# A plan that counts TensorE's instructions, and whole tiles stored at the end

## The chip, the cores and the metric

The kernel runs on one core of a Trainium2 chip. The metric is the device time of one execution in microseconds, the median over runs; lower is better. Before the change the median of three runs is 1213.6 us (1208.06, 1213.6, 1229.15).

## What is computed

A recurrent attention over 4 batches x 8 heads x 768 steps with a 40x40 state, then two feed-forward layers over the 3072 rows of 320 numbers:

```python
def _attn_ref(r, k, v, w, a, b):
    ...
    for t in range(S):
        y[:, :, t] = np.einsum('bhd,bhde->bhe', rt, state)
        Sa = np.einsum('bhde,bhe->bhd', state, at)
        state_decay = state * wt[:, :, None, :] - np.einsum('bhd,bhe->bhde', Sa, bt)
        state = state_decay + np.einsum('bhd,bhe->bhde', vt, kt)

x = attention as (B * S, H * D)                  # 3072 x 320
h = np.maximum(x @ w_in, 0.0); x = h * h @ w_out  # d_ff 2048
g = x @ w_gate; out = (g * sigmoid(g)) * (x @ w_val) @ w_out2   # d_ff 1536
```

## The kernel before

The recurrence is worked in chunks of 32 steps, so that almost everything is a product on TensorE: small float32 products of 16 to 64 columns on parts of the array (lines 802 to 1072, the stages x, v, p, u, s, t, z, c, y, S, k of the code). The profile shows a float32 product as two matmuls, each with a weight load. The two layers are split into high and low parts in the faster float32r format: the input products of the first layer (L460, 256 columns), its output products (L465, 320 columns), the same for the second layer (L460 with 512 columns, L1472).

All of this is put in order by a planner, `Plan`, when the program is built. Each step is an `op` with a cost for each engine that may take it, the keys it reads and writes, and a due time. `step` takes the engine that is free first, `choose` picks among the steps that are ready there, by due time, with rules that keep TensorE's clock up and avoid changes of the array's shape; `pe_time` gives a TensorE step its time. The result is one fixed order for each engine, in which the steps' functions emit their instructions. The first layer's products stand between the small products of the attention from about 185 us on; what is left of them when the attention is done covers the time in which the second layer's weights are loaded.

The second layer runs in six blocks of 512 rows (`pair2`): for each of 12 slices of 128 hidden columns, a gate product and a value product (`f_in`, eight matmuls each), the gate function on ACT and DVE (L1461, L1464), a split in gh (ACT, L436) and gl (DVE, L1130), and twelve output products into four tiles (`o_mm`, L1472). After the last slice ACT copies the four tiles out (`copy`, L436) and SP stores each in two halves of 64 rows (L1481).

At the program's end DVE collects range checks, one small product sums them (L1606), a flag is written (L1607), every engine loads it (L1608) and branches on it (L1609), and SP waits for the stores.

Below stand the functions that the change touches.

Of the kernel before, what the change touches and what calls it, by code (L numbers as in the profile page):

```python
# [21 lines left out]
DM = H * D  # L22
F1 = 2048
F2 = 1536
# [35 lines left out]


class Op:
    __slots__ = ("cost", "fn", "due", "seq", "need", "succ", "ready", "take", "give", "cols", "done", "eng", "tag", "mate", "claim", "dma", "mode", "act", "port", "lag", "leaves", "bulk")


class Free:
# [5 lines left out]
class Plan:  # L72
# [14 lines left out]
    def __init__(self):  # L87
        self.free = {e: 0.6 for e in (PE, ACT, DVE, POOL, SP)}
        self.dma = 0.0
        self.cand = {e: [] for e in self.free}  # L90
        self.writer, self.readers = {}, {}
        self.n = 0
        self.banks = {}
        self.kept = set()
        self.moe = []
        self.tick = {}
        self.now = 0.0
        self.held = {}
        self.left, self.last = {}, {}
        self.mode = None  # L100
        self.filler = None
        self.port = 0.0

    def op(self, cost, fn, r=(), w=(), due=0.0, dma=0.0, take=None, give=None, cols=0, tag="", mode=None, act=0, port=False, lag=0.0):
        o = Op()
# [1 line left out]
        self.n += 1  # L107
        o.dma, o.claim, o.mode, o.act, o.port, o.lag = dma, None, mode, act or cols, port, lag
        o.leaves = mode
        o.bulk = bool(cost) and SP in cost and not r  # L110
        o.succ, o.done, o.eng, o.mate = [], None, None, None
        o.ready = {e: 0.0 for e in (cost or self.free)}
# [91 lines left out]
    def choose(self, e, t):  # L204
        ok = [o for o in self.cand[e] if self.at(o, e) <= t + 0.02]
        ok.sort(key=lambda o: (o.due, o.seq))
        if e == PE and self.moe and ok:
            least = MOE_COLS if t > RAMP[0] else RAMP[1]

            def keeps(o):  # L210
                d = self.pe_time(o, t)
                return o.cols or self.moe_cols(t + d - self.TICK, t + d) + o.act >= least

            o = self.in_runs([o for o in ok if keeps(o)])
            if o is not None:
                return o
            if not keeps(ok[0]):
                for o in ok:
                    if o.cols:
                        return o  # L220
# [33 lines left out]
    def fill(self, now):  # L254
# [10 lines left out]
        if t < FILL_T[0] or t > FILL_T[1] or any(o.cols or t < FILL_T[2] for o in ok) or self.moe_cols(t + d - self.TICK, t + d) >= RAMP[2]:  # L265
            return False
        self.filler(b)
        self.busy(t, d, n)
        self.mode = None
        self.free[PE] = self.banks[b] = t + d  # L270
# [8 lines left out]
    def step(self):  # L279
# [17 lines left out]
        d = o.cost[e]  # L297
        if e == PE:
            d = self.pe_time(o, t)
            self.mode = o.leaves  # L300
            if o.act:
                self.busy(t, d, o.act)
# [29 lines left out]
        assert not any(self.cand.values())  # L332


MOE_COLS = 4400
BACKLOG = 1.2
SIDE = 4
# [35 lines left out]
def tile_kernel(ctx: ExitStack, tc: tile.TileContext, a: dict, out: bass.AP, nb: int, seq: int):  # L373
# [1069 lines left out]
    def pair2(P):  # L1443
# [5 lines left out]
        def f_in(kind):  # L1449
            w = two["w"]  # L1450
            in_products(two["p" + kind][b], f, two["xh"][B % 2], two["xl"][B % 2],
                        *((w.hg, w.lg, w.hlg) if kind == "g" else (w.hv, w.lv, w.hlv)))

        for kind in "gv":
            op({PE: 1.814}, lambda e, kind=kind: f_in(kind), ks, (("p" + kind, b),), due=due, cols=4096, tag="F2")
        kw = dict(due=due)

        def both(x):
# [9 lines left out]
        for t in range(4):  # L1468
# [5 lines left out]

            op({PE: 0.44}, o_mm, [("gh", n), ("gl", n)] + wk, (acc_keys[t],), due=due + 0.5, cols=960, tag="O")
            if f == nf - 1:
                op({ACT: 0.318}, lambda e, t=t: copy(e, two["o"][t], ACC2[t][:, :DM]), (acc_keys[t],), (("o2", t),),
                   due=due, tag="o")
                d = outv[2 * B + t // 2, t % 2]
                for r in range(2):  # L1480
                    op({SP: 0.42}, lambda e, t=t, d=d, r=r: nc.sync.dma_start(d[r], two["o"][t][64 * r:64 * r + 64]),  # L1481
                       (("o2", t),), (), due=due, dma=0.455, tag="dma")

    x2_load(0, NS + DELAY)
    for t in range(4):
# [200 lines left out]
```

## Time and profile before

| what | value |
|---|---|
| median of three runs | 1213.6 us |
| the profiled execution | 1212.33 us, span 1210.3 us, mean granted clock 0.968 |
| TensorE matmuls | 1113.8 us busy, 92% |
| VectorE, ScalarE, GpSimd | 639.5, 551.8, 97.1 us busy |
| chain that ended last | TensorE 67%, DMA 5%, DVE 5%, "issue" 3% |

The span runs from the first to the last instruction on the core's engines. Matmul and weight load are two instructions of TensorE's one queue (PE and PEld). An idle time that ends in "issue" is one in which the engine waited for nothing that the profile shows. Register, branch and semaphore instructions are not counted as busy. The rows themselves stand in a section below.

### The profile page before, as it was taken

How to read it: one execution, taken by the hardware profiler on the slowest of the kernel's cores; microseconds unless marked ns; L12 is line 12 of the kernel's file. 1: busy time of each engine (PE TensorE's matmuls, PEld its weight loads, DVE VectorE, ACT ScalarE, POOL GpSimd, SP SyncE). 2: the span in 40 equal slices, each digit the busy share in tenths (PEclk: the TensorE clock that was granted, in tenths of full speed). 3: DMA queues.
4: the chain of work that ended last, by engine and by line, in shares of the span. 5: the costliest groups of instructions: out<-in, count | busy, mean ns of one | idle time of the engine just before them, and what ended most of it. 6: DMA issues, size and time to landing. Idle time of an engine off the chain costs nothing.

```text
span 1210.3 us, 42859 instructions
## 1 busy us (share of the span) xinstructions
PE 1113.8 (92%) x18640; PEld 1011.7 (84%) x18640; DVE 639.5 (53%) x1496; ACT 551.8 (46%) x1275; POOL 97.1 (8%) x122
## 2 busy tenths in 40 slices
PE   7487978989889899999998999899999999999995
PEld 7376877888888798999898899888888888888884
DVE  4766885676657475856473422445334343434432
ACT  6344985555555464645453444654223222222221
POOL 0221331011011011210000000000000000000000
PEclk9788998999999999999999999899999999999998
DMA  5645664565655465544443322422101010100001
GB/s 137 159 112 155 163 172 121 141 179 142 172 134 148 136 175 157 151 130 99 109 102 77 69 58 65 132 86 83 35 7 26 18 27 22 27 23 1 22 1 25
DMA packets 171393, 114.96 MB, mean 95 GB/s; under 512 B 104092, under 2 KB 147644, under 8 KB 171196
## 3 DMA queue, kind: packets, MB, share of 16 engines
q1 hardware_dynamic: 168556, 110.52, 35.1%
q8 instruction: 148, 2.42, 0.9%
q10 hardware_dynamic: 2640, 1.61, 0.5%
q14 instruction: 49, 0.40, 0.1%
HBM read 88.35 MB, written 23.72 MB: 93 GB/s over the span
## 4 chain that ended last, share of the span: by engine, by line
PE 67%; DMA 5%; DVE 5%; issue 3%; SPq 2%; ACT 1%; DVEq 0%; ACTq 0%
PE ps L460 31%; PE ps L465 11%; PE ps L1472 10%; DMA ws<-f_moe_w_val 3%; SPq L723 2%; PE ps L1057 2%; PE ps L1038 2%; PE ps L1029 1%; PE ps L960 1%; PE ps L973 1%; PE ps L1072 1%; PE ps L802 1%; PE ps L999 1%; PE ps L868 1%; PE ps L954 1%
## 5 line engine op out<-in xcount | busy, mean ns | idle before, releaser
L1464 DVE TENSOR_TENSOR gr<-ps,gr 128x512 f32<-128x512 f32 x144 | 99.5, 692 | 168.4 <-PE ps L460 86.4
L1146 ACT ACTIVATE ps<-ps 128x512 f32<-128x512 f32 x192 | 111.6, 581 | 106.9 <-PE ps L460 104.3
L465 PE MATMUL ps<-o1h,gh 128*128 128x320 f32 x384 | 131.9, 343 | 4.0 <-ACT gh L436 3.9
L436 ACT CAST gh<-gr 128x512 fp32r<-128x512 f32 x72 | 44.8, 622 | 177.1 <-DVE gr L1464 177.1
L465 PE MATMUL ps<-o1l,gh 128*128 128x320 f32 x384 | 121.5, 316 | 2.7 <-issue 2.7
L465 PE MATMUL ps<-o1h,gl 128*128 128x320 f32 x384 | 122.5, 319 | 0.3 <-DVE gl L413 0.3
L460 PE MATMUL ps<-xh,w1h 128*128 128x256 f32 x384 | 117.1, 305 | 0.0
L460 PE MATMUL ps<-xl,w1h 128*128 128x256 f32 x384 | 109.9, 286 | 0.0
L460 PE MATMUL ps<-xh,w1l 128*128 128x256 f32 x384 | 109.8, 286 | 0.0
L413 DVE TENSOR_TENSOR gl<-ps,gh 128x512 fp32r<-128x512 f32 x96 | 65.8, 685 | 59.0 <-ACT gh L436 58.9
L1472 PE MATMUL ps<-o2h,gh 128*128 128x320 f32 x288 | 89.0, 309 | 1.9 <-ACT gh L436 1.4
L1472 PE MATMUL ps<-o2l,gh 128*128 128x320 f32 x288 | 88.8, 308 | 0.2 <-DVE o2l L1389 0.2
L1472 PE MATMUL ps<-o2h,gl 128*128 128x320 f32 x288 | 88.7, 308 | 0.2 <-DVE gl L1130 0.2
L465 PEld LDWEIGHTS ps<-o1h,gh 128*128 128x128 f32 x384 | 74.2, 193 | 9.8 <-ACT gh L436 4.7
L1461 ACT ACTIVATE gr<-ps 128x512 f32<-128x512 f32 x72 | 43.2, 599 | 81.2 <-PE ps L460 79.6
L465 PEld LDWEIGHTS ps<-o1h,gl 128*128 128x128 f32 x384 | 74.7, 195 | 4.6 <-issue 2.5
L460 PEld LDWEIGHTS ps<-xh,w1h 128*128 128x128 f32 x384 | 74.2, 193 | 1.9
L465 PEld LDWEIGHTS ps<-o1l,gh 128*128 128x128 f32 x384 | 74.8, 195 | 0.1
L1130 DVE TENSOR_TENSOR gl<-gr,gh 128x512 fp32r<-128x512 f32 x72 | 49.9, 693 | 47.1 <-ACT gh L436 47.0
L460 PEld LDWEIGHTS ps<-xl,w1h 128*128 128x128 f32 x384 | 74.5, 194 | 0.0
L460 PEld LDWEIGHTS ps<-xh,w1l 128*128 128x128 f32 x384 | 74.1, 193 | 0.0
L1282 PE MATMUL ps<-warm 128*128 128x256 f32 x302 | 50.6, 320 | 24.3 <-DVE ct L1213 14.5
(170 smaller groups left out, 2702.8 us busy)
## 6 DMA issues: line engine op xcount, KB each, us to landing
wakb<-in_wakb_dram SPq DMA_DIRECT2D x42, 422.5 KB
RB<-in_vr_e_dram SPq DMA_DIRECT2D x44, 208.0 KB
RH<-in_r_e_dram SPq DMA_DIRECT2D x90, 80.0 KB
cx<-in_moe_w_out_dram SPq DMA_DIRECT2D x21, 320.0 KB
room<-xt_d SPq DMA_DIRECT2D x36, 128.0 KB
cx<-in_moe_w_in_dram SPq DMA_DIRECT2D x15, 256.0 KB
xt_d<-yb SPq DMA_DIRECT2D x24, 160.0 KB
x_d<-room SPq DMA_DIRECT2D x24, 160.0 KB
```

The source lines that it names most:

```text
L413: nc.vector.tensor_sub(dst, full, hi.bitcast(F32))
L436: nc.scalar.copy(dst, src) if e == ACT else eng[e].tensor_copy(dst, src)
L460: nc.tensor.matmul(ps, w[:, c], x, start=(i == 0), stop=(i == len(seq_) - 1))
L465: nc.tensor.matmul(acc[t][:, :DM], g[:, half, ts], w[:, f, :], start=(f == 0 and i == 0), stop=(f == nf - 1 and i == 2),)
L723: o = att(cost, lambda e: queues[e].dma_start(dst(), src()), r, w, due=due, dma=dma, tag="dma")
L1038: nc.tensor.matmul(v[64 * p:64 * p + 64, jh, u], RW[:, 4 * jh + 2 * u + p], RB[:, :, s], start=True, stop=True)
L1130: op({POOL: t_pool(512), DVE: t_dve(512)}, lambda e: eng[e].tensor_sub(gl[n], two["gr"][n], gh[n].bitcast(F32)), (("gr", n), ("gh", n)), ( ...
L1146: op({ACT: 0.478}, lambda e, f=f: nc.scalar.activation(P1[b], P1[b], f), (), (("p", b),), due=due, tag="relu")
L1282: nc.tensor.matmul(PS[:, b, 0:256].rearrange("p (a b) -> p a b", a=2), warm, warm[:, None, :].to_broadcast([128, 2, 128]), start=True, sto ...
L1461: op({ACT: 0.478}, lambda e: nc.scalar.activation(both(two["gr"]), two["pg"][b], AF.Sigmoid), (("pg", b),), (("gr", n),), tag="sig", **kw)
L1464: op({DVE: 0.602}, lambda e, q=q: nc.vector.tensor_mul(both(two["gr"]), two[q][b], both(two["gr"])), ((q, b),), (("gr", n),), tag="u" + q, ...
L1472: nc.tensor.matmul(ACC2[t][:, :DM], x[n][:, t // 2, c], y[:, f, :], start=(f == 0 and i == 0), stop=(f == nf - 1 and i == 2))
```

## The change

`Plan` gets a count of TensorE's instructions. Each step carries `words`, a number by its kind: 16 for eight layer products, 128 or 192 for a stage of small products. `fetched` goes through the instructions of a step: whenever the count is 140 past a multiple of 256 a block is asked for, which is there 4.2 us later or 4.2 us after the block ahead of it; an instruction at 441, 697, ... waits for its block. `choose` drops steps that would wait 0.1 us or more so, unless all do, and `step` adds the wait to a step's time, both from 185 us of the plan's time on. In the second layer a finished tile is stored by one transfer of 128 rows. In the last block the copies alternate between ACT and DVE, a store may go to SP's or ACT's queue, and the last slice's gate and value products are due 0.6 earlier.

```diff
+        self.sent, self.blocks = 0, []
+
+    def fetched(self, n, t, d, keep):
+
+        a, b = self.sent, self.sent + n
+        blocks, wait = (self.blocks if keep else list(self.blocks)), 0.0
+        for x in range(a + 1, b + 1):
+            if x % BLOCK == ASKED:
+                blocks.append(max(t + wait + d * (x - a) / n, blocks[-1] if blocks else 0.0) + FETCH)
+            if x > LOADED and (x - LOADED) % BLOCK == 1:
+                wait += max(0.0, blocks[(x - LOADED) // BLOCK] - (t + wait + d * (x - a) / n))
+        if keep:
+            self.sent = b
+            return wait
+        k = (b - LOADED) // BLOCK + 1
+        if b > LOADED and k < len(blocks):
+            wait += max(0.0, blocks[k] - (t + wait + d) - (k * BLOCK + LOADED - b) / PACE)
+        return wait
...
+        o.words = WORDS.get(tag if isinstance(tag, str) else tag[0], 0)
...
+        if e == PE and t > FETCH_T:
+            ready = [o for o in ok if self.fetched(o.words, t, o.cost[PE], False) < STALL]
+            ok = ready or ok
...
             d = self.pe_time(o, t)
+            wait = self.fetched(o.words, t, d, True)
+            d += wait if t > FETCH_T else 0.0
...
+WORDS = {"F": 16, "O": 6, "F2": 16, "tp": 6, "u": 192, "s": 128, "t": 128, "v": 128, "p": 128, "y": 128, "x": 32, "c": 32,
+         "z": 8, "S": 8, "k": 8}
+BLOCK = 256
+ASKED = 140
+LOADED = 440
+FETCH = 4.2
+FETCH_T = 185.0
+STALL = 0.1
+PACE = 16.0
...
-            op({PE: 1.814}, lambda e, kind=kind: f_in(kind), ks, (("p" + kind, b),), due=due, cols=4096, tag="F2")
+            op({PE: 1.814}, lambda e, kind=kind: f_in(kind), ks, (("p" + kind, b),),
+               due=due - (0.6 if P == NB2 * nf - 1 else 0.0), cols=4096, tag="F2")
...
-                op({ACT: 0.318}, lambda e, t=t: copy(e, two["o"][t], ACC2[t][:, :DM]), (acc_keys[t],), (("o2", t),),
-                   due=due, tag="o")
-                d = outv[2 * B + t // 2, t % 2]
-                for r in range(2):
-                    op({SP: 0.42}, lambda e, t=t, d=d, r=r: nc.sync.dma_start(d[r], two["o"][t][64 * r:64 * r + 64]),
-                       (("o2", t),), (), due=due, dma=0.455, tag="dma")
+                end = B == NB2 - 1
+                op(({ACT: 0.43}, {DVE: 0.45})[t % 2] if end else {ACT: 0.318}, lambda e, t=t: copy(e, two["o"][t], ACC2[t][:, :DM]),
+                   (acc_keys[t],), (("o2", t),), due=due, tag="o")
+                op({SP: 0.6, ACT: 0.6} if end else {SP: 0.6},
+                   lambda e, t=t, d=outv[2 * B + t // 2, t % 2]: queues[e].dma_start(d, two["o"][t]),
+                   (("o2", t),), (), due=due, dma=0.6, tag="dma")
```

In the changed file the lines behind the new code stand 31 to 35 lower: L460 is L494 there, L465 L499, L868 L902, L954 L988, L999 L1033, L1472 L1507.

TensorE's order in the middle of the program, at about 302 to 310 us of the old trace; L999 is stage t, L868 stage p, L954 and L960 stage u, L1038 stage c, L802 stage x. Before:

```order
L999 MATMUL ps<-TV_157,KT_155 40x40 x16
L999 MATMUL ps<-TV_157,KT_156 40x40 x16
L1029 MATMUL ps<-ident,TV_157 104x128 x4
L460 MATMUL ps<-xh_111,w1h_99 128x256
...
L868 MATMUL ps<-P_129,vt 32x16 x32
L954 MATMUL ps<-TV_158,L_125 32x40 x16
L954 MATMUL ps<-TV_158,L_126 32x40 x16
L960 MATMUL ps<-ST_151,AB_148 64x40 x8
L960 MATMUL ps<-ST_152,AB_149 64x40 x8
L1038 MATMUL ps<-RB,RW_162 64x64 x8
L802 MATMUL ps<-AB_146,KB_135 64x64 x8
```

The same place in the changed kernel (L1007 is stage s, L836 stage x, L1072 stage c):

```order
L902 MATMUL ps<-P_129,vt 32x16 x32
L494 MATMUL ps<-xh_111,w1h_99 128x256
...
L836 MATMUL ps<-AB_145,KB_134 64x64 x8
L499 MATMUL ps<-o1h,gh_108 128x320
...
L1007 MATMUL ps<-UQ,P_128 32x40 x32
L499 MATMUL ps<-o1h,gh_108 128x320
...
L1033 MATMUL ps<-TV_157,KT_155 40x40 x16
L1033 MATMUL ps<-TV_157,KT_156 40x40 x16
L1063 MATMUL ps<-ident,TV_157 104x128 x8
L499 MATMUL ps<-o1h,gh_107 128x320
...
L1072 MATMUL ps<-RB,RW_162 64x64 x8
```

Stage t stood three steps ahead of p and u, with 16 input products of the first layer between; now p, s and t stand apart, each behind 3 to 16 of the first layer's products.

TensorE's last products. gh_107 with gl_109 is the last slice but one, gh_108 with gl_110 the last, wgh and wvh the weights of gate and value. Before:

```order
L460 MATMUL ps<-xl_13032,wghl 128x512
L1472 MATMUL ps<-o2h,gh_107 128x320
L1472 MATMUL ps<-o2l,gh_107 128x320
L1472 MATMUL ps<-o2h,gl_109 128x320
...
L460 MATMUL ps<-xh_13030,wvh_13038 128x512
...
L460 MATMUL ps<-xl_13032,wvhl 128x512
L1472 MATMUL ps<-o2h,gh_108 128x320
```

and in the changed kernel:

```order
L494 MATMUL ps<-xl_13032,wghl 128x512
L494 MATMUL ps<-xh_13030,wvh_13038 128x512
...
L494 MATMUL ps<-xl_13032,wvhl 128x512
L1507 MATMUL ps<-o2h,gh_107 128x320
L1507 MATMUL ps<-o2l,gh_107 128x320
L1507 MATMUL ps<-o2h,gl_109 128x320
...
L1507 MATMUL ps<-o2h,gh_108 128x320
```

The twelve output products of the last slice but one moved from between the gate and value products of the last slice to behind them.

SP's last instructions; o_13429 to o_13432 are the four tiles. Before:

```order
L1481 DMA out_dram<-o_13429 64x320 x2
L1481 DMA out_dram<-o_13430 64x320 x2
L1481 DMA out_dram<-o_13431 64x320 x2
L1481 DMA out_dram<-o_13432 64x320 x2
L1608 TENSOR_LOAD flag
```

and in the changed kernel, where the store of o_13431 stands on ACT:

```order
L1516 DMA out_dram<-o_13429 2x64x320
L1516 DMA out_dram<-o_13430 2x64x320
L1516 DMA out_dram<-o_13432 2x64x320
L1643 TENSOR_LOAD flag
```

Eight stores ahead of the flag's load became three; the tiles o_13430 and o_13432 are copied by DVE, behind its range checks.

## Rows read from the trace of the kernel before

**Rows 1.** The page: busy time by engine, and TensorE's instruction queue (packets, MB, share).

```profile
PE 1113.8 (92%) x18640; PEld 1011.7 (84%) x18640; DVE 639.5 (53%) x1496; ACT 551.8 (46%) x1275; POOL 97.1 (8%) x122
q8 instruction: 148, 2.42, 0.9%
```

**Rows 2.** Stretches: length, then busy us (instructions) of PE, PEld, DVE, ACT, POOL; clock.

```profile
219.90:765.00 545.10, 515.89 (x12337) 480.27 (x12337) 302.31 (x794) 283.54 (x664) 45.01 (x52) 0.98 0.48 124
765.00:830.00 65.00, 60.29 (x347) 54.63 (x346) 32.89 (x66) 35.30 (x80) 1.82 (x2) 0.95 0.37 108
830.00:1190.00 360.00, 360.00 (x1890) 316.27 (x1890) 147.89 (x222) 96.11 (x175) 0.00 (x0) 1.00 0.08 19
```

**Rows 3.** TensorE's waits, 219.9 to 765 us: total, times, longest.

```profile
PE ps L954 <- issue: 5.4, 4, 2.5
...
PE ps L465 <- issue: 0.4, 1, 0.4
```

**Rows 4.** Stretches up to and between waits that ended in issue.

```profile
361.98:368.69 6.71, 4.19 (x127) 3.74 (x128) 2.39 (x5) 1.78 (x4) 0.00 (x0) 1.00 0.77 182
0.00:191.60 191.60, 143.79 (x3281) 131.07 (x3282) 133.66 (x351) 120.29 (x319) 46.92 (x64) 0.89 0.58 149
191.60:693.23 501.63, 470.33 (x11858) 435.44 (x11858) 301.56 (x812) 261.40 (x627) 47.66 (x55) 0.98 0.52 132
```

**Rows 5.** Timeline of TensorE: start, us, line, tiles, shapes, count, idle before.

```profile
304.16 0.60 PE L999 MATMUL ps<-TV,KT 64*40 64x40 f32 x40 [0.76 <-issue]
...
308.85 0.77 PE L954 MATMUL ps<-TV,L 32*32 32x40 f32 x61 [0.91 <-issue]
...
313.13 0.27 PE L1029 MATMUL ps<-ident,TV 128*104 128x128 f32 x1 [1.03 <-issue]
...
353.87 0.73 PE L861 MATMUL ps<-p1t,L 32*32 32x16 f32 x64
354.52 0.39 PE L460 MATMUL ps<-xh,w1h 128*128 128x256 f32 x1
354.74 0.28 PE L460 MATMUL ps<-xl,w1h 128*128 128x256 f32 x1
354.86 0.28 PE L460 MATMUL ps<-xh,w1l 128*128 128x256 f32 x1
```

**Rows 6.** The end: three pieces of the chain, then rows of the timeline.

```profile
1180.99 1.75 PE ps L1472 x12
...
1195.49 0.70 DVE gr L1464
...
1196.21 0.63 ACT gh L436
...
1196.89 0.41 PE L1472 MATMUL ps<-o2h,gh 128*128 128x320 f32 x1 [1.44 <-ACT gh L436]
...
1197.61 0.42 PE L1472 MATMUL ps<-o2h,gl 128*128 128x320 f32 x1 [0.17 <-DVE gl L1130]
...
1198.07 1.74 ACT L436 COPY o<-ps 128x320 f32<-128x320 f32 x4 [1.23 <-PE ps L1472]
...
1200.09 0.14 DVE L1607 TENSOR_SCALAR flag<-cnt 1x1 int32<-1x1 f32 x1 [1.70 <-PE cnt L1606]
```

**Rows 7.** SP's last issues, and the lines of the flag (ns min/median/max, first to last start).

```profile
1198.52 6.09 SPq L1481 DMA_DIRECT2D out_dram<-o  x8
...
L1608 SPq TENSOR_LOAD <-flag x1: 737/737/737, 1204.7 to 1204.7; - x1
...
L1609 SPq EVENT_SEMAPHORE  x8: 17/17/17, 1208.3 to 1208.9; - x8
...
L1609 PEldq COMPARE_BRANCH  x1: 4095/4095/4095, 1200.9 to 1200.9; - x1
...
L1609 SPq COMPARE_BRANCH  x1: 50/50/50, 1205.8 to 1205.8; - x1
```

More of the change, by code (lines that the diff above doesn't have):

```diff
@@ L62 @@
 class Op:
-    __slots__ = ("cost", "fn", "due", "seq", "need", "succ", "ready", "take", "give", "cols", "done", "eng", "tag", "mate", "claim", "dma", "mode", "act", "port", "lag", "leaves", "bulk")
+    __slots__ = ("cost", "fn", "due", "seq", "need", "succ", "ready", "take", "give", "cols", "done", "eng", "tag", "mate", "claim", "dma", "mode", "act", "port", "lag", "leaves", "bulk", "words")
 class Free:
@@ L267, in fill @@
         self.filler(b)
+        self.fetched(4, t, d, True)
         self.busy(t, d, n)
```

## The prediction

> **What bounds the kernel now.** I read the page first, to see which engine is full: TensorE is busy 92% of the span, with as many weight loads as matmuls [rows 1]. Then the stretches, since that 92% is a mean: in 830 to 1190 us TensorE is busy 360 of 360 us at full clock and nothing but its own work can be saved there; in 219.9 to 765 us, where attention and the first layer share it, it is busy 515.9 of 545.1 us; in 765 to 830 us 60.3 of 65 [rows 2]. So some 29 us of idle TensorE lie in the middle stretch, the largest sum on the page outside the work itself. Third, what those 29 us wait for: nine groups end in "issue", from 5.4 us before L954 down to 0.4 us before L465, and these nine add up to 24.8 us [rows 3]. No other engine and no transfer that the profile shows ends them; what is left of the 29 is spread over tile data and gaps.
>
> What "issue" is here follows from counting. TensorE's own instruction queue carries 148 packets of 2.42 MB, 16 KB each, while loads and matmuls together are 37,280 [rows 1]: about 252 of them per packet. The long waits stand one such block apart: between the one that ends at 361.99 and the one that ends at 368.70 the trace has 127 matmuls and 128 loads, some 255 with one to spare for an instruction that the table does not list [rows 4]. So TensorE stands at block ends until the next 256 instructions have come. Where it does so at neighbouring ends, the resumptions at 304.16, 308.85 and 313.13 are 4.69 and 4.28 us apart [rows 5]: when it only waits for blocks, one comes per about 4.3 us. The work between them, 308.85 - 0.91 - 304.16 = 3.78 us and 3.25 us, is what small products make of 256 instructions: 64 matmuls of L861, 128 instructions, go by in 0.65 us (353.87 to 354.52), while eight of L460, 16 instructions, take about 1 us (0.12 each) [rows 5].
>
> [...]
>
> **The change, part by part.**
>
> *Counting.* From its time 185 on, the plan gives each TensorE step a number of instructions, keeps the last end of a block's load, and passes over steps that would stall 0.1 us or more. The first place where TensorE's order differs is at 219.9 us of the old trace, so the waits before it stay, and 24.8 us is all that can be gained. The rows of the order show how: where three groups of small products stood nearly together, L465 and L460 stand between them.
>
> Would all of it go? I laid the block ends along both orders: each group priced by its rows in the old trace, a block asked for at instruction 140 of the one before (the change's own constant), 4.3 us until it is there or after the block ahead of it, and a wait where the work in between is shorter. For the old order this gives 24.3 us in 25 places, against 24.8 measured, so the arithmetic is fit for use. For the new order it gives 2.3 us if the ends lie where the plan puts them, but 15.2 us in 16 places if they lie where the chip has them. They differ because the plan counts products and loads alone, and the chip's blocks hold the semaphore instructions too. The rows show the drift: up to the wait at 191.6 us there are 3281 + 3282 = 6563 loads and matmuls, and the plan has its block end at 441 + 24 x 256 = 6585, 22 later; up to the wait at 693.2 us there are 6563 + 2 x 11,858 = 30,279, and its end is at 441 + 117 x 256 = 30,393, 114 later [rows 4]. The plan thus guards a window that slides off by a tenth to a third of its length. Spreading small products helps there too, only less: 24.3 - 15.2 = 9.1 us. With 4.2 us per block it is 20.9 to 12.5, with 4.5 us 31.7 to 20.7, so 8.4 to 11 us. I take 9.1.
>
> *More changes of kind.* In matmuls 3133 to 16,356 the new order has 338 changes of tile shape for 330. A first matmul behind another shape comes late: L460 at 354.52 is followed after 0.22 us, the next after 0.12 [rows 5]. Eight times 0.1 to 0.2 us is about 1.3 us. Both orders have put out the same number of first-layer products when the last product of attention comes, so the reserve that covers the weight loads of 765 to 830 us is neither larger nor smaller, and a gain before 765 moves that stretch forward whole.
>
> *Whole tiles.* Each block's eight stores of 80 KB become four of 160 KB on SP. For the first five blocks this is nothing: they lie beside 360 us in which TensorE does not wait [rows 2]; without that cover the saving would be some 0.6 us per store on SP.
>
> *The last products.* Before, the last value product came behind twelve output products, and TensorE then waited 1.44 us for gh and 0.17 more for gl: at 1195.49 L1464 began (0.70), the cast to gh followed (0.63), and at 1196.89 TensorE went on [rows 6]. Now both input products come first, and twelve output products, 1.75 us [rows 6], cover that chain. The value product ends 1.75 us earlier, so gh is ready at 1195.1 and gl at 1195.8; TensorE reaches the last twelve at 1195.5 and may wait 0.1 for gl. Its last product comes 1.4 + 0.4 - 0.1 = 1.7 us earlier.
>
> *Copies and stores at the end.* The last copy then ends near 1198.1 and the flag, which ends 0.42 us behind it now (1199.81 and 1200.23), is there near 1198.5 [rows 6]. Before, that did not matter: SP's eight stores ran 1198.52 to 1204.61, and only then did SP load the flag (1204.7), branch (1205.8) and go on at 1208.3; the others had branched at 1200.9 [rows 7]. This chain of SP alone set the end, 5.6 us behind its load. Now SP has three stores, ACT one. The third goes out when its tile is copied, at 0.6 to 0.76 us, so SP loads the flag near 1198.8, 5.9 us earlier. Against that: SP's branch took 2.5 us beside nobody, TensorE's 4.1 us beside three others [rows 7]; now all branch together, so 1.6 us may be lost, and eight waits on half as many stores give 0.4 back. The gain is 5.9 - 1.6 + 0.4 = 4.7 us. Bounds: 6.3 if SP's branch keeps its 2.5 us, 3.1 if the last store on SP is held up by a further 1.6 us. [...]
>
> **Sum.** The profiled execution took 1212.3 us (span 1210.3 and 2.0 around it), 0.1% under the median of 1213.6. 1212.3 - 9.1 + 1.3 - 4.7 = 1199.8; from the median 1201.1. I say 1201, with 1195 to 1207 as the likeliest case's own range.
>
> **Rivals.** First, the drift does not matter, or the semaphore instructions are fewer than I think: 22.5 us of waits go, and the time is 1212.3 - 22.5 + 1.3 - 4.7 = 1186.4, or 1187.7 from the median, just over 2% faster. For it speaks that the plan's own places would keep only 2.3 us; against it the count of [rows 4]. Second, the waits only move: the instructions are the same, and where one group is pushed off, it meets the next end. Then the tail alone remains, 1212.3 + 1.3 - 4.7 = 1208.9. The 16 places speak for it, that the sum over them falls by a third against. Third, slower: steps of the recurrence (u, s, t) that the plan passes over for a block come late, and their chain through DVE and ACT becomes what TensorE waits for. In the new order such steps stand up to some 7 us later in TensorE's work between 400 and 450 us. To be slower by 2% this needs 24 + 12.5 = 37 us of new waits; now waits of TensorE on data are about 4 us in that stretch and DVE is busy 302 of 545 us [rows 2], so there is room. It would be some 1240.
>
> **Chances.** Likeliest 0.62, first rival 0.15, second 0.18, slower 0.05. Two percent, 24 us, is about what can be told from no change here, where three runs of the old kernel lie 21 us apart. Faster by over 2% is the first rival, near its edge, with a little luck of the likeliest: 0.14. Slower 0.04. Within 0.82. The range takes in the second rival and its lost tail, 1211, and the first, 1187.
>
> **What would show it.** In the new trace the "issue" waits of TensorE from 219.9 us to the last attention product should sum to 13 to 17 us, with long ones left late in the stretch; under 6 us means the drift is harmless, over 22 that waits moved. Data waits there should stay under 6 us. The last attention product, that of L1057, should end 6 to 10 us earlier. In the tail, TensorE's wait ahead of the last twelve products should be under 0.3 us, SP's load of the flag should come within 1 us of the others', and the end 4 to 6 us behind the flag. I would be wrong above all if blocks come slower or faster than 4.3 us when data transfers are spread differently.

## The result and the profile after

The changed kernel takes 1226.4 us (median of 12 runs, 1218.4 to 1234.7), the kernel before 1216.4 us beside it (12 runs, 1207.3 to 1229.2): a ratio of 1.008 with a 95% interval of 1.005 to 1.011. It is some 10 us slower, where 1201 us and at most 1211 were predicted.

The profiled execution of the changed kernel spans 1228.9 us, 18.6 more than the one of before. Cut at the same matmuls of TensorE's order (the 4030th, the 16,229th, the last output product), the two spans differ by +2.6 us up to 222 us, where the order is the same, by +10.3 in the middle (526.6 us before, 536.9 after), by -1.3 from there to the last output product, and by +7.1 from its start to the end (11.2 before, 18.3 after). So there are two losses, one in the middle and one at the end, and each has its own rows.

**The middle.** The row of its stretch, to be read beside [rows 2] (length, then busy us and instructions of PE, PEld, DVE, ACT, POOL; clock, DMA share, GB/s), before and after:

```profile
219.90:746.50 526.60, 497.70 (x12197) 462.65 (x12198) 296.31 (x782) 272.27 (x642) 45.01 (x52) 0.98 0.48 124
```

```profile
222.50:759.40 536.90, 505.35 (x12202) 469.59 (x12200) 300.46 (x786) 271.39 (x639) 42.79 (x50) 0.97 0.48 121
```

TensorE is busy 7.7 us longer with the same products, at a lower mean clock, and idle 31.5 us instead of 28.9. What it waits for (total, times, longest), first more rows of before, beside [rows 3], then after:

```profile
PE ps L868 <- issue: 5.2, 2, 2.7
PE ps L999 <- issue: 3.9, 3, 2.2
PE ps L973 <- issue: 3.4, 3, 3.0
...
PE ps L868 <- DMA P<-pt_d: 1.8, 3, 0.8
```

```profile
PE ps L1091 <- DVE ut L1036: 5.2, 1, 5.2
PE ps L1091 <- issue: 4.6, 3, 2.8
PE ps L1072 <- issue: 3.8, 2, 2.0
PE ps L1007 <- issue: 3.5, 4, 1.2
PE ps L1063 <- DVE TV L1018: 3.3, 1, 3.3
PE ps L494 <- issue: 2.3, 2, 2.1
PE ps L1091 <- DMA RH<-in_r_e_dram: 2.0, 2, 1.5
PE ps L1033 <- issue: 1.5, 1, 1.5
PE ps L1063 <- ACT TV L1017: 1.2, 1, 1.2
PE ps L1091 <- DVE ST L1045: 1.1, 1, 1.1
```

All rows that end in issue, the waits for a block of instructions, sum to 17.4 us, against 24.8 before. All others, the waits for data, sum to 13.8, against 3.4. The longest of these others can be followed through three engines. SP issues two loads of wakb, the 22nd and 23rd of 46, back to back at 306.14 us; in the order before the same two went out at 280.26 and 290.08:

```profile
303.80 1.63 SPq L757 DMA_DIRECT2D room<-xt_d  x3
305.47 0.57 SPq L757 DMA_DIRECT2D TV<-in_v_t_dram  x1
306.14 0.93 SPq L757 DMA_DIRECT2D wakb<-in_wakb_dram  x2
```

```profile
280.26 0.51 SPq L723 DMA_DIRECT2D wakb<-in_wakb_dram  x1
...
290.08 0.34 SPq L723 DMA_DIRECT2D wakb<-in_wakb_dram  x1
```

The load is late twice over. By its semaphore it is complete at 314.48, 8.3 us behind its issue (8.1 in both other executions of this order that are shown below), while half of the 29 wakb loads between 220 and 700 us are complete within 5.1 us, within 4.7 before. DVE stands 5.87 us at the scan that needs the load; the sum `ut` (L1036) stands behind the scan in DVE's order, and TensorE stands 5.18 us for `ut`:

```profile
314.57 0.71 DVE L808 TENSOR_TENSOR_SCAN DT<-wakb,c 104x264 f32<-104x264 f32 x1 [5.87 <-DMA wakb<-in_wakb_dram]
...
316.42 0.49 DVE L1036 TENSOR_TENSOR ut<-ps,ST 104x320 f32<-104x320 f32 x1
```

```profile
318.96 0.36 PE L1091 MATMUL ps<-RH,SX 40*40 40x32 f32 x8 [5.18 <-DVE ut L1036]
```

This wait costs twice. The clock falls to its lower level (0.50) while TensorE stands, and stays there for 10 us of work behind it:

```profile
308.00:318.00 10.00, 5.78 (x112) 5.07 (x110) 4.04 (x9) 2.37 (x7) 0.00 (x0) 1.00 0.73 199
318.00:328.20 10.20, 9.24 (x202) 8.61 (x204) 7.22 (x17) 3.70 (x11) 2.42 (x3) 0.50 0.35 74
329.00:339.00 10.00, 10.00 (x260) 9.15 (x248) 8.49 (x24) 6.84 (x19) 1.56 (x2) 1.00 0.62 141
```

In the middle the lower level is granted for 37 us after the change and 17 us before.

**The end.** The last products came as wanted: 451.2 us from the cut behind the attention to the last output product instead of 452.5, and the only wait near them is 0.4 us of a weight load for gl (1.44 and 0.17 us of TensorE's in [rows 6]). The flag is written at 1211.77. From there on nothing goes as in [rows 7]: SP's load of the flag comes 1.3 us behind the others', and the end 17 us behind the flag, where within 1 us and 4 to 6 us were expected. These are SP's stores (start, us from the first issue to the end of the last), the flag's loads and the branches (ns min/median/max, first to last start):

```profile
1210.04 3.25 SPq L1516 DMA_DIRECT2D out_dram<-o  x3
```

```profile
L1643 PEldq TENSOR_LOAD <-flag x1: 2014/2014/2014, 1212.0 to 1212.0; - x1
L1643 SPq TENSOR_LOAD <-flag x1: 2544/2544/2544, 1213.3 to 1213.3; - x1
...
L1644 SPq EVENT_SEMAPHORE  x8: 17/17/17, 1223.6 to 1227.5; - x8
...
L1644 SPq COMPARE_BRANCH  x1: 50/50/50, 1216.3 to 1216.3; - x1
```

The loads of a flag of four bytes take 1.9 to 2.5 us; SP's took 0.74 [rows 7]. SP's way behind its branch takes 7.3 us (1216.3 to 1223.6; 2.5 before), and then it still waits 3.9 us, since the stores are not done. Three stores took SP 3.25 us to issue, 1.1 us each. What the DMA engines do in this time (queue, packets, MB, share of 16 engines), after from 1209.5 to 1227 us, and before from 1198 to 1209:

```profile
q1 hardware_dynamic: 390, 0.49, 8.6%
q10 hardware_dynamic: 130, 0.16, 2.6%
```

```profile
q1 hardware_dynamic: 640, 0.66, 26.3%
```

Before, eight stores of 64 rows make 640 packets on SP's queue, 64 rows and 16 small packets for each (128 packets of this time are under 512 bytes). After, three stores of 128 rows make 390: 128 rows and two small packets each (8 are under 512 bytes, with the store of ACT's queue). The shares show how many DMA engines carry the whole tiles: 8.6 + 2.6% of 16 engines over 17.5 us is 31.4 us of packets, and the stores' packets run from 1211.2 to 1226.7, 15.5 us, so two engines are at work in the mean. The stretch's row has 49 GB/s in its last column, loads of instructions included:

```profile
1211.50:1226.50 15.00, 0.19 (x2) 0.11 (x2) 0.15 (x1) 0.00 (x0) 0.00 (x0) 0.64 0.15 49
```

The whole tile's target is 2 x 64 x 320, as the order of SP shows: two outer pieces, two small packets and two engines. Whether the pieces are the cause is tried below.

### The profile page after: what moved, and what is told of

The parts are those of the page before. It is cut to its first block, busy times and chain, and to the rows that moved or that the text cites. A ratio compares the mean times of both kernels' runs of the same rounds, so it can differ in the third digit from the quotient of the medians.

```text
span 1228.9 us, 42819 instructions
## 1 busy us (share of the span) xinstructions
PE 1126.2 (92%) x18640; PEld 1024.3 (83%) x18640; DVE 645.0 (52%) x1502; ACT 549.3 (45%) x1269; POOL 96.4 (8%) x122
## 4 chain that ended last, share of the span: by engine, by line
PE 71%; DMA 8%; issue 2%; DVE 2%; ACT 2%; SPq 2%; POOL 0%; DVEq 0%; ACTq 0%; POOLq 0%
PE ps L494 32%; PE ps L499 12%; PE ps L1507 10%; PE ps L1091 2%; DMA ws<-f_moe_w_val 2%; PE ps L1072 2%; PE ps L994 2%; SPq L757 2%; DMA wakb<-in_wakb_dram 1%; PE ps L1106 1%; PE ps L1063 1%; PE ps L988 1%; PE ps L1033 1%; PE ps L836 1%; PE ps L952 1%
## 5 line engine op out<-in xcount | busy, mean ns | idle before, releaser
L499 PE MATMUL ps<-o1h,gh 128*128 128x320 f32 x384 | 132.7, 346 | 5.0 <-ACT gh L470 4.9
L499 PE MATMUL ps<-o1l,gh 128*128 128x320 f32 x384 | 122.6, 319 | 3.2 <-DVE DT L808 3.2
L499 PE MATMUL ps<-o1h,gl 128*128 128x320 f32 x384 | 123.0, 320 | 0.3 <-DVE gl L447 0.3
L494 PE MATMUL ps<-xh,w1h 128*128 128x256 f32 x384 | 118.4, 308 | 0.0
L494 PE MATMUL ps<-xl,w1h 128*128 128x256 f32 x384 | 109.8, 286 | 2.8 <-issue 2.3
L494 PE MATMUL ps<-xh,w1l 128*128 128x256 f32 x384 | 109.4, 285 | 0.0
L1507 PE MATMUL ps<-o2h,gh 128*128 128x320 f32 x288 | 88.9, 309 | 0.7 <-ACT o2h L470 0.7
L1507 PE MATMUL ps<-o2l,gh 128*128 128x320 f32 x288 | 88.8, 308 | 0.2 <-DVE o2l L1423 0.2
L1507 PE MATMUL ps<-o2h,gl 128*128 128x320 f32 x288 | 88.7, 308 | 0.1
L499 PEld LDWEIGHTS ps<-o1h,gh 128*128 128x128 f32 x384 | 75.6, 197 | 9.0 <-ACT gh L470 5.7
L499 PEld LDWEIGHTS ps<-o1h,gl 128*128 128x128 f32 x384 | 75.6, 197 | 4.6 <-issue 3.3
L1316 PE MATMUL ps<-warm 128*128 128x256 f32 x302 | 53.2, 334 | 25.1 <-DVE ct L1247 14.3
L494 PEld LDWEIGHTS ps<-xh,w1h 128*128 128x128 f32 x384 | 73.9, 192 | 2.7
L499 PEld LDWEIGHTS ps<-o1l,gh 128*128 128x128 f32 x384 | 75.9, 198 | 0.1
L494 PEld LDWEIGHTS ps<-xh,w1l 128*128 128x128 f32 x384 | 73.9, 192 | 2.4 <-issue 2.4
L494 PEld LDWEIGHTS ps<-xl,w1h 128*128 128x128 f32 x384 | 74.2, 193 | 1.0 <-DVE xl L1132 1.0
```

The lines of the kernel that those rows point to most:

```text
L494: nc.tensor.matmul(ps, w[:, c], x, start=(i == 0), stop=(i == len(seq_) - 1))
L499: nc.tensor.matmul(acc[t][:, :DM], g[:, half, ts], w[:, f, :], start=(f == 0 and i == 0), stop=(f == nf - 1 and i == 2),)
L1316: nc.tensor.matmul(PS[:, b, 0:256].rearrange("p (a b) -> p a b", a=2), warm, warm[:, None, :].to_broadcast([128, 2, 128]), start=True, sto ...
L1507: nc.tensor.matmul(ACC2[t][:, :DM], x[n][:, t // 2, c], y[:, f, :], start=(f == 0 and i == 0), stop=(f == nf - 1 and i == 2))
```

## The experiments

The expectations call the theories by letters. A: the end is long because of the shape of the whole tile's store. B: the middle is long because loads on SP land too late for the new order. D: any order that the planner newly makes brings waits of its own. S: the stalls that the old plan did not know kept TensorE later than its data. Every ratio is to the kernel before, run beside it.

### The two halves of the change

One kernel has the counting alone, one the end alone. Against the change, the first is

```diff
-                end = B == NB2 - 1
-                op(({ACT: 0.43}, {DVE: 0.45})[t % 2] if end else {ACT: 0.318}, ...
-                op({SP: 0.6, ACT: 0.6} if end else {SP: 0.6}, ...
+                op({ACT: 0.318}, ...
+                for r in range(2):
+                    op({SP: 0.42}, ...
```

with the 0.6 of the last products' due time gone too, and the second

```diff
-            ready = [o for o in ok if self.fetched(o.words, t, o.cost[PE], False) < STALL]
-            ok = ready or ok
...
-            wait = self.fetched(o.words, t, d, True)
-            d += wait if t > FETCH_T else 0.0
```

> The counting alone: the plan counts TensorE's instructions, the stores and the last products stay as before. TensorE's order up to the last block is that of the change. Theory A (the loss of 10 us lies at the end, where the whole-tile stores move data at a seventh of the DMA engines' share and hold SP up): this is 4 to 8 us faster than before, and the end, from the last product to the end of the span, is the 11 us of before. Theory B (the loss lies in the middle: 7.4 us of block waits are gone, but 9.6 us of waits on data and some 6.7 us of a lower clock came, late wakb loads above all): this is 4 to 9 us slower than before, with 12 to 18 us of issue waits and 10 us or more of data waits between 220 us and the last attention product. Both can hold: then 0 to 6 us slower.

> The end alone: whole-tile stores, two queues and copies by two engines in the last block, the last products reordered, no counting. Theory A: the end is 16 to 19 us long from the last product (11 before), so in spite of 1.7 us won by the products the time is 4 to 7 us longer than before. Theory B: the long end of the one profiled execution is chance, and this is 3 to 5 us faster than before, as the prediction had it.

The counting alone takes 1220.6 us, ratio 1.002 (0.999 to 1.005); in its profile the middle is 534.9 us and the end, from the last output product on, 11.3. The end alone takes 1216.7 us, 0.999 (0.996 to 1.003); its middle is 523.4 us and its end 18.1. So the long middle belongs to the counting, the long end to the stores, and neither gains anything.

### The shape of the store

The end alone, with the tiles stored in halves as before but still from two queues:

```diff
-                op({SP: 0.6, ACT: 0.6} if end else {SP: 0.6},
-                   lambda e, ...: queues[e].dma_start(d, two["o"][t]), ...
+                for r in range(2):
+                    op({SP: 0.42, ACT: 0.42} if end else {SP: 0.42},
+                       lambda e, ...: queues[e].dma_start(d[r], two["o"][t][64 * r:64 * r + 64]), ...
```

> The end alone as in the other run, but each tile stored in two halves of 64 rows as before: eight stores on two queues, copies by two engines, last products reordered, no counting. Theory A (the shape of the whole-tile store, 2 x 64 rows, is what makes it slow): the end from the last product falls to 7 to 9 us, and the time is 4 to 6 us under before. If instead it is the second queue or DVE's copies that lengthen the end, this is as slow as with whole tiles.

It takes 1206.3 us, 0.989 (0.984 to 0.993), and its end 8.8 us. A repetition, with the profile of a second execution:

> The same kernel as the one with the change's tail in half-tile stores and no counting, second of its call instead of last. By its profile it is the kernel before with 2 to 3 us less at the end (8.8 instead of 11.2), so 1213 to 1216 if its first time (1206) was luck of its place, 1206 if something else in it is faster.

1209.4 us, 0.995 (0.991 to 0.999), end 8.9. The profiles show 2.3 us at the end and 1.8 by the products' order, so some 4 us; both medians show more (11 and 6), and what the rest is stays open. To part the shape from the size of the store, whole tiles went to 128 neighbouring rows. The rows of this kernel's output stand in another order than they should, so its time alone is read:

```diff
-                   lambda e, t=t, d=outv[2 * B + t // 2, t % 2]: queues[e].dma_start(d, two["o"][t]),
+                   lambda e, t=t, d=out[(4 * B + t) * 128:(4 * B + t + 1) * 128]: queues[e].dma_start(d, two["o"][t]),
```

> The change's tail alone, without the counting, and each whole tile goes to 128 neighbouring rows of the output (so the rows of the output are permuted) instead of to two pieces of 64 rows. Size, number and queues of the stores stay: 160 KB, three on SP and one on ACT. Theory A, that the two pieces as the outer step put the store on 2 of the 16 DMA engines: now 16 carry it, each flag load is back at 0.5 to 0.8 us, last product to end 7.5 to 9 us instead of 18, time within 3 us of the version with half-tile stores, about 11 us under the kernel before. Rival, that 160 KB stores or two queues are slow by themselves: last product to end stays near 18 us and the time near the kernel before.

The end takes 8.4 us, the shortest of all, a load of the flag 0.76 us again, and the issue of SP's three stores 1.72 us instead of 3.2. The DMA row from 1198.5 to 1207 us now has 16 small packets for each 128 rows, 3 x 144 = 432, and in seven slices of 0.21 us 90% or more of the 16 engines are busy:

```profile
q1 hardware_dynamic: 432, 0.49, 16.2%
```

Size, number and queues are those of the version with an end of 18.1 us, so the two outer pieces are the cause. The medians show only part of it: 1215.0 us, 0.996 (0.993 to 0.999), against 0.999, some 4 us where the ends differ by 9.7. Why is open; the twelve executions of this kernel alone lie 14 us apart. The half-tile stores in the whole change:

> The whole change, only the second layer's stores go out in halves of 64 rows. Theory A: last product to end 9 us instead of 18.3, the time 9 to 10 us under that of the change, so equal to the kernel before within 4 us. The order of the middle is the change's own, so the waits there should come again if they belong to the order: some 17 us for blocks, 10 to 14 us for data, 30 us or more of low clock. If the data waits were an accident of one execution they are 4 to 8 us and the time is 5 us or more under the kernel before.

1216.4 us, 0.998 (0.995 to 1.002), 10 us under the change; end 8.9 us. Its middle is again long, 533.1 us, with the waits of the change at the same places: 5.7 us for `ut` behind the scan of wakb, 3.1 for TV. These waits belong to the order, not to one execution.

### Blocks that follow the chip's

```diff
-BLOCK = 256
+BLOCK = 255
```

With the old end, and with half-tile stores:

> The counting alone, with blocks of 255 instructions instead of 256 in the plan, which follows the chip's block ends to within a few instructions, since TensorE's semaphore instructions are about one in 260 of its stream. If the drift is what left 17 us of block waits in the change, issue waits between 220 us and the last attention product fall to 2 to 7 us. If block waits were all that matters there, the time is 15 to 20 us under before; if data waits and the clock take back what is won (theory B), it is within 6 us of before in spite of the few block waits. If the drift is not the cause, issue waits stay at 13 us or more.

> Counting with blocks of 255, which follow the chip's blocks, and the second layer's stores in halves: both parts as they were meant. If the counting were worth its tally, the middle is 12 us shorter than before and the time about 1195. If data waits take it back, as in the run with 255 alone (9.7 us for blocks, 17.8 for data), the time is that run's less the tail's gain of 2 to 9 us: 1204 to 1213, no better than the version with half-tile stores and no counting (1206).

1215.9 us, 0.998 (0.995 to 1.001), and 1215.3 us, 0.997 (0.994 to 1.001). Block waits are 9.6 and 13.4 us, less than the 16.2 to 18.6 of the change's order. By itself this does not show the drift of the plan's ends, since some orders with blocks of 256, below, have 6.1 to 9.7. Other waits are 17.8 and 20.2, the longest 6.2 and 6.4 us for the load of p1t. Nothing is won.

### Loads earlier, and what is chance

In the change with half-tile stores the loads of wakb were made due earlier; the same edit in the kernel before, without counting and with the old end; and the kernel before once more, unchanged.

```diff
-            load(lambda: WA[wa(g)], ..., due - 1, 1.8)
+            load(lambda: WA[wa(g)], ..., due - 1.6, 1.8)
```

> The change with half-tile stores, and the planner is told that the load of wakb is due 1.6 chunks ahead of its scan instead of 1. Theory B, that the counting's gain is lost because loads on SP come late for the new order and DVE stands at the scan: waits for data fall from 13 to 4 to 8 us, low clock under 25 us, blocks 10 to 13 us by the tally (9.5), the time 8 to 12 us under the change with half-tile stores. Rival D, that any order which the planner has not had before brings its own waits: data waits 10 us or more again, at other places, and the time within 4 us of the change with half-tile stores.

> The same kernel as the one with the counting, half-tile stores and wakb's loads 1.6 chunks ahead, first of its call instead of last. If its order is what made it fast: 1201 within 4 us, middle 518 to 524 us, blocks 7 to 10 us, and again about 5 us less between the last attention product and the second layer. If its place in the call did: 1208 or more.

> The kernel before, only with wakb's loads due 1.6 chunks ahead: a new order without counting and with the old end. By the tally 19.6 us of block waits instead of 24.3. Theory B (late loads of wakb are what new orders lose by): data waits 4 us or less, time 3 to 6 us under before. Rival D (any order new to the chip brings waits for loads that land late): data waits 8 us or more, time equal to before or up to 6 us over it.

> The kernel before, unchanged, as the last of its call: what the comparison makes of no difference. All theories: ratio 1.000 within 0.004. If the last place of a call is favoured: 0.99. The profile gives a second execution of the old order: block waits 15 to 20 us if the 25.0 of the first were high by chance, 24 to 26 if they belong to the order.

With counting and the earlier loads it takes 1200.9 us, 0.988 (0.983 to 0.993), and repeated 1200.6 us, 0.988 (0.981 to 0.994): the fastest kernel here, faster than either theory had it, 17.5 and 14.8 us under the kernel before. But not as theory B had it. The waits for data did not fall; they are 16.9 us, and two rows hold most of it:

```profile
PE ps L1072 <- ACT RW L470: 7.0, 1, 7.0
PE ps L1033 <- ACT TV L1017: 4.1, 1, 4.1
```

The first is the same mechanism with another load. ACT stands 8.26 us for a piece of the second layer's weights, and RW is behind it:

```profile
254.87 0.48 ACT L457 ACTIVATE cx<-cx 128x320 int32<-128x320 uint32 x1 [8.26 <-DMA cx<-in_moe_w_gate_dram]
255.26 1.05 ACT L470 COPY RW<-ps 104x512 f32<-104x512 f32 x2
```

What it gains against the kernel before: block waits of 6.5 us in a middle of 520.0 us (521.8 in the repetition; some 2 us of either is work that falls outside it, as said below the table); 6.6 us less from there to the last product (445.8 instead of 452.4), of which 1.8 are the products' order, and 3.9 a wait of L465 for gh that does not occur; and 2 us at the end. Without counting the same due time gives 1213.1 us, 0.997 (0.994 to 1.001).

The kernel before against itself gave 1.000 (0.995 to 1.004). Its second profile has 19.5 us of block waits where [rows 3] had 24.8.

### What brings the waits for data

Four kernels, all with half-tile stores: one in which the plan prices stalls but passes over nothing (`STALL = 0.1` became `STALL = 1e9`), and three in which it lets every load land 1.5 us later, with counting, without, and with blocks of 255:

```diff
-            end = self.dma = max(self.dma, t + d + 0.585) + o.dma
+            self.dma = max(self.dma, t + d + 0.585) + o.dma
+            end = self.dma + 1.5
```

> The change with half-tile stores, but no step is passed over for a block's end: the plan counts and adds the stall to a step's time, and chooses as before. If the passing over brings the waits for data: they fall to 4 to 8 us, block waits are 18 us or more, time 1209 to 1215 as the version without counting. If every new order brings them: 10 us or more again, time 1215 or more.

> The change with half-tile stores, and the planner lets every load land 1.5 us later than it did. Theory B in its general form (the new orders lose by loads that land later than the plan has them): waits for data under 8 us, low clock under 20 us, blocks 12 to 18 us by the tally (15.7), time 1200 to 1208. If the waits for data are not from loads: 12 us or more again, time 1212 to 1220.

> The same 1.5 us, half-tile stores, without the counting. Theory B: the old order had few waits for data (4 to 8 us) and gains little by it; blocks 20 to 26 us by the tally (25.8), time 1208 to 1216, so over the version with counting by 4 to 10 us. If the gain is that of a lucky order and not of counting with loads in time: equal to the version with counting within 4 us, or below it.

> The 1.5 us for every load, half-tile stores, and counting with blocks of 255, which follow the chip's. Theory B: waits for data under 8 us where the same counting without the 1.5 us had 18 to 19, blocks 6 to 12 us, time 1195 to 1203, the fastest of all. Rival: 15 us of waits for data again, time 1210 or more.

Without passing over: 1221.9 us, 1.006 (1.002 to 1.009), and the waits for data are the highest of all, 21.6 us, now on loads directly; so they come without the passing over too. That the block waits fall to 6.1 us although nothing avoids them fits a simple tie between the two, that a block arrives while TensorE stands for data; no run tried it by itself.

```profile
PE ps L895 <- DMA p1t<-p_d: 6.6, 4, 5.0
PE ps L1072 <- DMA RB<-in_vr_e_dram: 6.6, 2, 4.2
PE ps L952 <- ACT KT L470: 2.9, 1, 2.9
PE ps L988 <- DMA TV<-in_v_t_dram: 2.2, 1, 2.2
```

The kernels with later loads take 1235.5, 1223.4 and 1222.4 us (1.013, 1.006, 1.004), but most of that is ahead of the middle: they are at the 4030th matmul at 236 to 241 us instead of 222. In their middles the waits for data are 18.3 us with counting, 5.7 without, and 9.6 with blocks of 255. The first pair speaks against theory B, since 1.5 us more for each load do not spare the counting its waits. It does not end it: with blocks of 255 they are half of the 20.2 us above, and the load of wakb in the change landed over 3 us later than others do, so 1.5 us need not bring every load in time. Last, 1.2 us of slack for whatever reaches TensorE from 185 us on:

```diff
+            if e == PE and p.eng not in (None, PE) and p.done > 185.0:
+                o.ready[e] = max(o.ready[e], p.done + self.HOP[p.eng][e] + 1.2)
```

> The change with half-tile stores, and from 185 us on the planner lets every result of another engine and every load reach TensorE 1.2 us later than it did. Theory S (the stalls that the old plan does not know made TensorE later than the plan, so data was there; with the stalls in the plan that slack is gone): with the slack given back the waits for data are under 8 us, block waits 10 to 15 us by the tally (10.5), the sum of both under 22 us, low clock under 20 us, the middle 515 to 523 us, time 1200 to 1208. If slack is not what is missing: waits for data 12 us or more again, the sum 26 us or more, middle 530 us or more, time 1214 or more.

> The same 1.2 us of slack and half-tile stores, without the counting. Theory S: little to gain, since the slack was there: waits for data 3 to 7 us, blocks 20 to 27 us by the tally (29), the middle 523 to 530 us, time 1209 to 1216, and 5 to 10 us over the version with counting. If both are equal within 4 us, the counting is worth nothing even with the slack given back.

They take 1231.4 us, 1.016 (1.010 to 1.021), and 1227.5 us, 1.014 (1.010 to 1.019). Theory S is not borne out either: the waits for data stay at 12.2 us with counting, and without it they are 17.3. The slack was given to what reaches TensorE, not to loads that DVE and ACT wait for. This last kernel also shows that a new order without any counting can have them.

### All middles side by side

The length from the 4030th to the 16,229th matmul and TensorE's busy time in it, from the stretch's row, and its waits that end in issue and in anything else, summed over the rows of that view:

| order of the middle | length | issue | else | busy |
|---|---|---|---|---|
| before, six executions | 523.3 to 526.7, mean 525.0 | 15.4 to 24.8, 19.7 | 3.4 to 8.3, 6.5 | 496.1 to 500.4, 498.1 |
| the change's, three | 533.1 to 536.9, 535.0 | 16.2 to 18.6, 17.4 | 12.4 to 15.4, 13.9 | 501.1 to 505.4, 503.3 |
| blocks of 255, two | 524.2, 536.5 | 9.6, 13.4 | 17.8, 20.2 | 496.1, 502.1 |
| counting, loads of wakb earlier, two | 520.0, 521.8 | 6.5, 7.4 | 16.9, 20.1 | 496.1, 493.7 |
| priced, nothing passed over | 535.3 | 6.1 | 21.6 | 507.1 |
| counting, loads 1.5 us later | 531.1 | 9.7 | 18.3 | 502.6 |
| 255, loads 1.5 us later | 521.3 | 12.1 | 9.6 | 499.2 |
| counting, slack | 536.2 | 17.2 | 12.2 | 505.7 |
| no counting, loads of wakb earlier | 527.0 | 16.3 | 10.5 | 500.1 |
| no counting, loads 1.5 us later | 522.0 | 19.8 | 5.7 | 496.3 |
| no counting, slack | 538.0 | 16.4 | 17.3 | 503.1 |

The six executions of before are those of the kernel before (two) and of the versions with the end alone (four), which have its middle. Issue and else together are 23 to 28 us in all six, and 22 to 34 in the fourteen others. On the whole the counting lowers the first and raises the second. The two matmuls do not bound the same products in every order. With loads 1.5 us later some 6 to 8 us of this work, with the earlier loads of wakb and counting some 2 us, falls outside them (estimates from the products that differ, at what such products take in the trace of before). With that added back, orders without counting lie between 523 and 538 us, orders with it between 522 and 539: which order it is matters more than whether stalls are counted.

## Why the prediction was wrong

The profiled execution took 1230.8 us where the sum gave 1199.8. Of these 31 us 18.1 are the middle (+10.3 measured, -9.1 + 1.3 forecast), 10.5 the end with the products' order (+5.8, -4.7), and 2.6 lie ahead of the middle, where the order is the same.

**The base of the counting's term.** The step "24.3 - 15.2 = 9.1 us" stood on one execution with 24.8 us of block waits, and the tally was held fit for use because it gave 24.3. That execution was the highest of six of the same order; the others have 15.4 to 20.5 and the mean is 19.7, so the agreement was luck. No run shows the place 140 at which the tally lets a block be asked for, it is the change's constant. For the new order the tally was not far off: 15.2 forecast, 17.4 measured, within the 13 to 17 us that "What would show it" named but for 0.4. So the term is 2.3 us, not 9.1. The profiled time lay under the median all the same (1212.3 of 1213.6), which hid that its waits were untypical.

**The drift** was right, and the traces show it directly: with the semaphore instructions of TensorE's queue counted too, 239 of 242 block waits of 0.5 us or more, between 185 and 770 us in all twenty traces, stand at the 194th or 195th instruction of 256. With loads and matmuls alone that place slides, before from the 164th at 191.6 us to the 72nd at 693.2. The first rival (all waits go) was rightly set low.

**The waits for data** were the step that failed in the middle. They "should stay under 6 us"; they are 13.9 in the mean of three executions, 7.4 more than before, and TensorE's busy time is 5.2 us longer. Most of that is the clock: the lower level is granted for 33 us in the mean of these three and for 18 in the mean of the six before, and 13 of the 15 us more begin at or just behind a wait for data. The prediction had this mechanism as its third rival, with u, s and t late through DVE and ACT, at about 37 us of new waits and a chance of 0.05 for slower by 2%. It came at a fifth of that size, its longest wait, 5.2 us, through a late load for which DVE stood 5.87 us, so the likeliest case should have carried some of it as a cost. No term of the sum did, and none priced the clock behind a wait. -2.3, +7.4 and +5.2 make the 10 us by which the middles differ; the medians show it smaller, 3 us in the counting alone and about 8 between the two versions with half-tile stores and the new end.

**The changes of kind**, +1.3 us, show as 0.7 us of busy time at most: two executions with 27.3 us at the lower level each, with half-tile stores without and with the counting, are busy 500.4 and 501.1 us.

**The second rival**, that waits only move, was nearest for the middle: issue and else together are 26.2 us in the mean before and 31.3 after. Where it was wrong is that a moved wait is not as cheap as a block's; TensorE stands longer at one place (5.2 us in the change's profile, 3.0 at most in that of before), and the clock stays low longer behind it (10 us, against 3.4 each time in the middle of before, and 3.4 to 6.8 at the block waits of the change).

**The end.** The products' order gave what was worked out, 1.8 us in the mean of six executions with it against four without (forecast 1.7). "Whole tiles ... for the first five blocks this is nothing" holds: from the cut behind the attention to the last product the end alone takes 450.4 us with whole tiles, 450.8 with halves. The failed step is the last block's: the sum priced the store's issue, 0.6 to 0.76 us (1.1 here), and not how long it takes to land, 15.5 us for the four tiles, and the landing sets the end. With the new end and stores that 16 engines carry, the end is 8.4 to 9.2 us against 11.2; the forecast's 4.7 us, of which 1.7 are the products', meant 8.2. With two engines it is 18.2, 7 us longer than before. The order's rows showed the target's 2 x 64 x 320 before the prediction was made, and the prediction did not ask what that shape does to the landing. The 1.6 us for branching beside the others were near: SP's way behind its branch is 3.7 us with half-tile stores (2.5 before).

**What stays open:** why orders with counting have more waits for data. They come without the passing over, and neither 1.5 us more for each load nor 1.2 us of slack takes them away at blocks of 256; whether more would, was not tried. That an order without counting has them as well (17.3 us) speaks for D, the 5.7 us of another against it as a rule; a third has 10.5. And it stays open why the version with half-tile stores gained more than its profile shows.

## What to carry over

A wait that is removed from one engine's order is a gain only if the next thing on that engine is there: before counting it, list what the new order will wait for, above all the loads that other engines stand for on its behalf (here 5.87 us of DVE at wakb), and price the clock behind a long wait (here 10 us at 0.50). Take the base of a term from several executions when the term is under one per cent of the time. And of a transfer at the end count the landing, not the issue: the same four tiles landed in 15.5 us as 2 x 64 rows and in 2.0 us as 128 rows.

## What the runs showed of the hardware

Two DMA engines took 15.4 and 15.5 us for 0.66 MB in rows of 1280 bytes; 16 took 2.0 us for the same tiles whole and 2.9 in halves. With two at work, the flag's loads take 1.5 to 2.5 us instead of 0.5 to 0.95, and SP's way behind its branch 7.1 and 7.3 us instead of 2.5 to 4.1. What joins the stores and these reads was not tried by itself.

Six executions of the same middle had between 15 and 25 us of block waits and between 10 and 27 us at the lower clock level; what makes them differ was not found. The clock fell at or just behind about half of TensorE's 194 waits of a microsecond or more in the middles of all twenty traces, and at all 24 of 3 us or more; after the 9.6 us wait of the repeated fast version it stayed low for 17 us:

```profile
251.50:268.60 17.10, 11.20 (x219) 10.17 (x221) 5.86 (x14) 7.20 (x16) 3.29 (x3) 0.50 0.49 134
```
